# Batch 1's MLP: the leaky slope on ScalarE instead of a product of the weights, and a deeper queue between the products

## The chip, the core and the metric

The kernel runs on one core of one Trainium2 chip. TensorE (PE) multiplies matrices, VectorE (DVE), ScalarE (ACT) and GpSimd (POOL) work elementwise, SyncE (SP) issues most of the DMAs. Times are device microseconds (us) of one execution; less is better.

## The reference

Two steps follow one another: a long convolution, gated by x, and an MLP with a leaky slope.

```python
# 2 batches, seq 12480, d_model 128
h_filt = (np.maximum(pos_emb @ w1, 0.0) @ w2) * np.exp(-0.01 * pos)[:, None]
u = x * v
L = 2 * S
y = np.fft.irfft(np.fft.rfft(u, n=L, axis=1) * np.fft.rfft(h_filt, n=L, axis=0)[None], n=L, axis=1)[:, :S, :]
attn = x * y
# MLP, d_ff 2048, over all 24960 tokens
h = attn.reshape(B * S, D) @ w_in
out = np.maximum(0.01 * h, h) @ w_out
```

## The kernel before

The convolution is a transform of two stages, written as matrix products, with the spectra of batch 0, of batch 1 and of the filter made on the chip. Batch 0's transforms come first (to about 360 us). From then on PE runs the MLP; batch 1's transforms are cut into small pieces (`conv1`, a generator) that the MLP's loop calls between its steps during batch 0's blocks. All of them have run by the time that batch 1's first block begins. The last step of each transform back is made tile by tile in `front(t)`: a tile has 390 tokens, and there are 32 for each batch. `join(t)` makes the sum and the difference cp of what was loaded (L500, L501, on POOL), `front(t)` transposes x (L708), copies it (xs, L710, ACT), multiplies by the last matrix (yp, L716, PE), gates (zf, L719, DVE) and splits the result into two parts, zh (rounded to fp32r, L724, ACT) and zl (the residual, L725, POOL).

The MLP goes over 50 blocks of tokens, 25 for each batch, most of 512 columns (`widths`; batch 1's last two have 352), and over 16 slices of d_ff in each. `m1(k, f)` makes the hidden slice: three passes in fp32r, w_in_h by zh, w_in_h by zl, w_in_l by zh, into one of three PSUM buffers mh. ACT takes the Relu to rh (L737), DVE the residual rl (L738), both from mh. `m2(k, f, r)` adds three more passes to the block's accumulator acc. The slope is not applied elementwise: since max(0.01 h, h) is 0.99 relu(h) + 0.01 h, the kernel keeps 0.99 w_out as w_out_h and w_out_l, and the product wc = 0.01 w_in w_out, and each block begins its accumulator with three passes of z by wc (L748 to L750). `weights()` makes these in the stage before the MLP.

The order is written out by hand. PE gets `m1` of a slice and, DEEP slices later, its `m2`:

```python
pend.append((k, f, m1(k, f)))
if len(pend) > DEEP:
    m2(*pend.pop(0))
```

DEEP is 2, and rh and rl have DEEP + 2 buffers. The steps of `join` and `front` are tied to slices by `ends`: the last part of a tile's front stands behind slice 13 of the block ahead of the one that needs it, or earlier. `finish(k)` copies acc, transposes it back and stores it during the next block. Every engine carries out its instructions in this order.

The matrix of the last-but-one step is held twice: mi2 for batch 0, and mi for batch 1, split once into mi_h and mi_l (L275, L276) in chunk 6 of the first stage. Tiles with the tags bin1, hd and ct1 in the pool sb1 (two, two and one buffers) serve batch 1's transforms.

Of the kernel before, what the change touches and what calls it, by code (L numbers as in the profile page):

```python
# [8 lines left out]
F32 = mybir.dt.float32  # L9
# [3 lines left out]
AF = mybir.ActivationFunctionType  # L13
ALU = mybir.AluOpType
# [10 lines left out]
WIDE = 512  # L25
# [3 lines left out]
def tile_conv_mlp(ctx, tc, x, v, pos_emb, w1, w2, w_in, w_out, cf, cr, cg, cb, ci, cw, out):  # L29
    nc = tc.nc  # L30
    B, S, D = x.shape
# [22 lines left out]
    w_out_h = const.tile([128, NF, D], F32R, name="w_out_h")  # L54
# [50 lines left out]
    def run(g):  # L105
        for _ in g:
            pass
# [50 lines left out]
    with tc.manual_schedule():  # L158
# [17 lines left out]
        def mult_a(c):  # L176
            ft, (xt, vt) = got.pop(c)
            nc.gpsimd.tensor_tensor(out=xt, in0=xt, in1=vt, op=ALU.mult)
            u1[c] = ft, xt

        with ExitStack() as st:
# [4 lines left out]
            mi = s0.tile([128, 2, 128], F32, tag="mi", name="mi", bufs=1)  # L186
# [4 lines left out]
            def load_pos(q):  # L191
                pos_t[q] = sba.tile([NA, 2, PQ, FO], F32, tag="pos", name="pos")
                load_tokens(pos_t[q], pos_emb, q * PQ, PQ)

            def load_a(c):
                ft = sba.tile([NA, MC, 2 * NA], F32, tag="ft", name="ft", bufs=5)
                nc.sync.dma_start(out=ft, in_=cf[:, c * MC:(c + 1) * MC, 0])
                xt = sba.tile([NA, 2, MC, D], F32, tag="xt", name="xt", bufs=3)
                vt = sba.tile([NA, 2, MC, D], F32, tag="vt", name="vt", bufs=3)
                load_tokens(xt, x[0], c * MC, MC)  # L200
                load_tokens(vt, v[0], c * MC, MC)
                f_t[c], xv_t[c] = ft, (xt, vt)
                if c < 2:
                    f1_t[c] = sba.tile([NA, MC, 2 * NA], F32, tag="f1", name="f1", bufs=3)
                    nc.sync.dma_start(out=f1_t[c], in_=cf[:, c * MC:(c + 1) * MC, 1])
# [56 lines left out]
            for c in range(NC0):  # L262
                if c + 3 < NC0:
                    load_a(c + 3)
                    if (c + 3) * MC % PQ == 0:
                        load_pos((c + 3) * MC // PQ)
                if c == 2:
                    nc.sync.dma_start(out=mb, in_=cb)
                    nc.sync.dma_start(out=mi, in_=ci)
                    for s in range(2):  # L270
                        for ri in range(2):
                            nc.sync.dma_start(out=mi2[HB * s:HB * s + HB, ri], in_=ci[HB * ri:HB * ri + HB, s])
                if c == 6:
                    for m, mh, ml in ((mb.rearrange("p s r q -> p s (r q)"), mb_h, mb_l), (mi, mi_h, mi_l)):
                        nc.scalar.copy(mh, m)  # L275
                        nc.vector.tensor_tensor(out=ml, in0=m, in1=mh, op=ALU.subtract)  # L276
                for f in late:
                    f()
                late = []
                uh, ft, f1 = uh_t.pop(c), f_t.pop(c), f1_t.pop(c)  # L280
                nxt = prep(c + 2) if c + 2 < NC0 else iter(())
                o = sba.tile([NA, 2, MC, 2, C0], F32, tag="o", name="o")

                def store(m0, n, o, c=c):
                    for ri in range(2):
                        r0 = HB * ri + c * MC + m0
                        nc.sync.dma_start(out=scr1[r0:r0 + n].rearrange("m k e -> k m e"),
                                          in_=o[:, ri, m0:m0 + n].rearrange("a m s d -> a m (s d)"))
                if c == 7:
                    w22 = s0.tile([128, D], F32, tag="mi", name="w22", bufs=1)  # L290
                    for i in range(2):
                        nc.sync.dma_start(out=w22[64 * i:64 * i + 64, :], in_=w2)
                if c == NC0 - 3:
                    fetch_a(0)

                    bin0 = s0.tile([128, MC1 * 4 * NA], F32, tag="s0", name="bin0", bufs=3)[
                        :, :KC * 2 * C0].rearrange("p (k s e) -> p k s e", k=KC, s=2)

                def early():
                    for ri in range(2):  # L300
                        rows = slice(HB * ri, HB * ri + HB - DIR * MC)
                        nc.sync.dma_start(out=bin0[rows], in_=scr1[rows, :KC, :].rearrange("p k (s e) -> p k s e", s=2))

                def direct(m, o, c=c):
                    for ri in range(2):
                        r0 = HB * ri + c * MC + m
                        nc.sync.dma_start(out=bin0[r0:r0 + 1], in_=o[:KC, ri, m])
                if c == NC0 - 1:
                    mult_a(0)
                for mm in range(MC):  # L310
                    a = psa.tile([NA, 2, 512], F32, tag="a", name="a", bufs=3)
                    for p, f, n in ((0, ft, NA), (1, f1, ROWS)):
                        for ri in range(2):
                            nc.tensor.matmul(a[:, p, C0 * ri:C0 * ri + C0], f[:n, mm, NA * ri:NA * ri + NA],  # L314
                                             uh[:n, p, mm], start=True, stop=True)
                    run(add_sub(sba, a[:, 0, :2 * C0], a[:, 1, :2 * C0], o[:, :, mm, 0, :], o[:, :, mm, 1, :],
                                lambda t: t.rearrange("a (r e) -> a r e", r=2), 2))
                    next(nxt, None)
                    if c >= NC0 - DIR:
                        direct(mm, o)  # L320
                    if c == NC0 - 1 and mm == EARLY:
                        early()
                    if c == NC0 - 1 and mm == MC - 1:
                        store(0, MC, o)
                if c < NC0 - 1:
                    late.append(lambda store=store, o=o: store(0, MC, o))
# [3 lines left out]
        psc = {}  # L330
# [136 lines left out]
        ld, z, acc = {}, {}, {}  # L467
# [36 lines left out]
        with ExitStack() as st:  # L504
# [73 lines left out]
            def two(tag):  # L578
                return [psb.tile([128, 512], F32, tag=tag, name=tag + "p", bufs=2) for _ in range(2)]
# [36 lines left out]
            for c in range(NCH):  # L616
# [16 lines left out]
                hp = two("h")  # L633
                for ri in range(2):
                    for k in range(n):
                        i, j = 64 * (k % 2), ri * n // 2 + k // 2
                        nc.tensor.matmul(hp[k % 2][:, D * j:D * j + D], es[i:i + 64, k // 2, ri, :], w22[i:i + 64, :],
                                         start=True, stop=True)
# [41 lines left out]
        ps = ctx.enter_context(tc.tile_pool(name="ps", bufs=1, space=bass.MemoryType.PSUM, reuse_waits="tile"))  # L680
# [11 lines left out]
        at0 = [sum(widths[:i]) for i in range(len(widths) + 1)]  # L692
# [34 lines left out]
        def m1(k, f):  # L727
            w = widths[k]
            zh, zl = (i[:, :w] for i in z[k])
            hp = ps.tile([128, WIDE], F32, tag="mh", name="mh", bufs=3)[:, :w]  # L730
            fs = slice(f * 128, f * 128 + 128)
            nc.tensor.matmul(hp, w_in_h[:, fs], zh, start=True, stop=False)  # L732
            nc.tensor.matmul(hp, w_in_h[:, fs], zl, start=False, stop=False)  # L733
            nc.tensor.matmul(hp, w_in_l[:, fs], zh, start=False, stop=True)  # L734
            rh = sm.tile([128, WIDE], F32R, tag="rh", name="rh", bufs=DEEP + 2)[:, :w]
            rl = sm.tile([128, WIDE], F32R, tag="rl", name="rl", bufs=DEEP + 2)[:, :w]
            nc.scalar.activation(out=rh, in_=hp, func=AF.Relu)  # L737
            nc.vector.scalar_tensor_tensor(out=rl, in0=hp, scalar=0.0, in1=rh, op0=ALU.max, op1=ALU.subtract)  # L738
            return rh, rl

        def m2(k, f, r):
            rh, rl = r
            w = widths[k]
            if f == 0:
                zh, zl = (i[:, :w] for i in z[k])
                acc[k] = ps.tile([128, WIDE], F32, tag="acc", name="acc", bufs=2)
                ap = acc[k][:, :w]
                nc.tensor.matmul(ap, wc_h, zh, start=True, stop=False)  # L748
                nc.tensor.matmul(ap, wc_h, zl, start=False, stop=False)
                nc.tensor.matmul(ap, wc_l, zh, start=False, stop=False)  # L750
            ap = acc[k][:, :w]
            nc.tensor.matmul(ap, w_out_h[:, f, :], rh, start=False, stop=False)  # L752
            nc.tensor.matmul(ap, w_out_h[:, f, :], rl, start=False, stop=False)  # L753
            nc.tensor.matmul(ap, w_out_l[:, f, :], rh, start=False, stop=(f == NF - 1))  # L754

# [28 lines left out]
                r0 = n + ROWS * NB + 2 * mp  # L784
                nc.sync.dma_start(out=out[None, r0:r0 + 2, :], in_=os_[ROWS:, 0])

        ZB, DEEP = 3, 2

        first = [next(pieces_of(t))[0] for t in range(total)]
        ends, e = {}, NTL * NF  # L790
# [68 lines left out]
        for q in pend:  # L859
            m2(*q)  # L860
# [69 lines left out]
```

## Time and profile before

| | us |
|---|---|
| median of 3 runs | 1763.5 |
| lowest and highest run | 1760.52, 1767.96 |
| profiled execution | 1763.3 |
| its span, first to last instruction | 1761.5 |
| PE busy | 1691.1 (96%) |
| DVE busy | 924.5 (52%) |
| ACT busy | 862.2 (49%) |
| POOL busy | 566.5 (32%) |

Busy times are summed over the span, and the share that PE is busy rises from the transforms at the start to the MLP. Matmuls overlap one another, so a busy PE says only that one was always under way. The rest of the time between span and execution lies outside the first and the last instruction.

### The profile page before, as it was taken

The page shows a single profiled execution, that of the slowest core. Times are in us where ns is not written, and L with a number is a line of the kernel's source. Part 1 is how long each engine was busy: PE and PEld are TensorE (multiplying, and loading weights), DVE is VectorE, ACT ScalarE, POOL GpSimd, SP SyncE. Part 2 cuts the span into 40 slices and gives each one's busy share as a digit, 9 for nine tenths or more (in the row PEclk, how much of TensorE's full clock was granted, in tenths as well). Part 3 has the DMA queues.
Part 4 walks back from the last instruction along what each step waited for, and adds up shares of the span by engine and source line. Part 5 has one row for each costly group of instructions (what it writes and reads, how often), then busy time and mean ns, then how long its engine had stood idle before and what let it go on. Part 6 is the DMA issues. An engine that isn't in the chain of part 4 may idle for free.

```text
span 1761.5 us, 25712 instructions
## 1 busy us (share of the span) xinstructions
PE 1691.1 (96%) x9234; PEld 1398.1 (79%) x9234; DVE 924.5 (52%) x1487; ACT 862.2 (49%) x1673; POOL 566.5 (32%) x474
## 2 busy tenths in 40 slices
PE   6788999699999999999999999999999999999998
PEld 5687555488888888888888888988888888888888
DVE  3566788545454555565555554444444444444444
ACT  1222455234444466667666665444444444444444
POOL 3453122223322166566555653121112111202110
PEclk9889999889999999999999999999999999999999
DMA  8898999766656565656555642221212121212110
GB/s 226 244 269 256 325 327 342 255 179 185 178 150 178 134 176 142 173 150 176 165 140 144 168 131 88 67 70 47 61 50 69 46 59 56 64 38 72 51 30 19
DMA packets 147683, 251.04 MB, mean 143 GB/s; under 512 B 10835, under 2 KB 96930, under 8 KB 144484
## 3 DMA queue, kind: packets, MB, share of 16 engines
q1 hardware_dynamic: 127412, 223.71, 45.4%
q10 hardware_dynamic: 20144, 25.69, 4.1%
q8 instruction: 73, 1.20, 0.3%
q14 instruction: 54, 0.44, 0.1%
HBM read 165.86 MB, written 83.43 MB: 142 GB/s over the span
## 4 chain that ended last, share of the span: by engine, by line
PE 77%; DMA 9%; DVE 6%; issue 3%; SPq 2%; POOL 1%; ACT 1%; ACTq 0%; DVEq 0%; POOLq 0%
PE mh L732 10%; PE acc L753 10%; PE acc L754 10%; PE acc L752 9%; PE mh L734 9%; PE mh L733 9%; PE yp L716 6%; PE cv L132 4%; PE cv L351 2%; DMA scr<-o 2%; PE op L776 2%; DVE ta L126 1%; PE a L314 1%; DMA ft<-in_cf_dram 1%; PE xp L708 1%
## 5 line engine op out<-in xcount | busy, mean ns | idle before, releaser
L738 DVE SCALAR_TENSOR_TENSOR rl<-mh,rh 128x512 fp32r<-128x512 f32 (+3 forms) x800 | 540.7, 678 | 614.7 <-ACT rh L737 612.0
L737 ACT ACTIVATE rh<-mh 128x512 fp32r<-128x512 f32 (+3 forms) x800 | 470.2, 589 | 374.1 <-PE mh L734 352.2
L732 PE MATMUL mh<-zh,w_in_h 128*128 128x512 f32 (+3 forms) x800 | 327.1, 409 | 0.0
L753 PE MATMUL acc<-rl,w_out_h 128*128 128x512 f32 (+3 forms) x800 | 309.9, 387 | 1.4 <-DVE rl L738 1.4
L752 PE MATMUL acc<-rh,w_out_h 128*128 128x512 f32 (+3 forms) x800 | 310.8, 389 | 0.3 <-ACT rh L737 0.3
L734 PE MATMUL mh<-zh,w_in_l 128*128 128x512 f32 (+3 forms) x800 | 310.3, 388 | 0.0
L754 PE MATMUL acc<-rh,w_out_l 128*128 128x512 f32 (+3 forms) x800 | 310.1, 388 | 0.0
L733 PE MATMUL mh<-zl,w_in_h 128*128 128x512 f32 (+3 forms) x800 | 309.3, 387 | 0.2 <-DVE zl L725 0.2
L725 POOL TENSOR_TENSOR zl<-zf,zh 128x390 fp32r<-128x390 f32 (+24 forms) x110 | 67.9, 630 | 700.3 <-ACT zh L724 699.8
L753 PEld LDWEIGHTS acc<-rl,w_out_h 128*128 128x128 f32 x800 | 150.6, 188 | 36.6 <-DVE rl L738 5.5
L734 PEld LDWEIGHTS mh<-zh,w_in_l 128*128 128x128 f32 x800 | 150.6, 188 | 31.8
L752 PEld LDWEIGHTS acc<-rh,w_out_h 128*128 128x128 f32 x800 | 150.7, 188 | 31.5 <-ACT rh L737 1.4
L754 PEld LDWEIGHTS acc<-rh,w_out_l 128*128 128x128 f32 x800 | 150.6, 188 | 30.8
L733 PEld LDWEIGHTS mh<-zl,w_in_h 128*128 128x128 f32 x800 | 151.1, 189 | 23.9 <-DVE zl L725 0.4
L732 PEld LDWEIGHTS mh<-zh,w_in_h 128*128 128x128 f32 x800 | 151.0, 189 | 22.5
L716 PEld LDWEIGHTS yp<-g,cp 98*128 98x128 f32 x1024 | 124.4, 192 | 6.4 <-POOL cp L500 1.2
L716 PE MATMUL yp<-g,cp 98*128 98x97 f32 (+1 forms) x1024 | 123.6, 274 | 1.0 <-POOL cp L500 0.9
L724 ACT CAST zh<-zf 128x390 fp32r<-128x390 f32 (+24 forms) x111 | 37.6, 378 | 156.0 <-DVE zf L719 156.0
L500 POOL TENSOR_TENSOR cp<-cin 98x512 f32<-98x512 f32 x63 | 84.4, 1339 | 17.0 <-DMA cin<-scr 17.0
L99 ACT COPY a1s<-a 98x384 f32<-98x384 f32 x64 | 30.7, 480 | 111.7 <-PE a L314 67.9
L314 PE MATMUL a<-uh,ft 98*98 98x192 f32 x256 | 61.7, 370 | 24.5 <-DVE o L103 21.4
L438 POOL TENSOR_TENSOR usp<-usp,hd 128x512 f32<-128x512 f32 (+1 forms) x50 | 65.3, 1307 | 60.0 <-ACT usp L436 41.9
(127 smaller groups left out, 2109.3 us busy)
## 6 DMA issues: line engine op xcount, KB each, us to landing
cin<-scr SPq DMA_DIRECT2D x64, 392.0 KB
hd<-hspec SPq DMA_DIRECT2D x48, 512.0 KB
g<-in_cg_dram SPq DMA_DIRECT2D x65, 300.1 KB
scr<-o SPq DMA_DIRECT2D x32, 588.0 KB
bin<-scr SPq DMA_DIRECT2D x23, 768.0 KB
scr1b<-o SPq DMA_DIRECT2D x32, 392.0 KB
xm<-in_x_dram SPq DMA_DIRECT2D x65, 192.0 KB
hspec<-hs ACTq DMA_DIRECT2D x48, 256.0 KB
```

Source lines behind the costliest of these rows:

```text
L132: nc.tensor.matmul(dst, u, w, start=(i == 0), stop=(i == 2))
L314: nc.tensor.matmul(a[:, p, C0 * ri:C0 * ri + C0], f[:n, mm, NA * ri:NA * ri + NA], uh[:n, p, mm], start=True, stop=True)
L500: eng.tensor_tensor(out=o1, in0=c0, in1=c1, op=ALU.subtract)
L716: nc.tensor.matmul(yp[:, at:at + n], ci_t[:, r, m, p, :], g[:, r, p, m, :n], start=(r == 0), stop=(r == 1))
L732: nc.tensor.matmul(hp, w_in_h[:, fs], zh, start=True, stop=False)
L733: nc.tensor.matmul(hp, w_in_h[:, fs], zl, start=False, stop=False)
L734: nc.tensor.matmul(hp, w_in_l[:, fs], zh, start=False, stop=True)
L737: nc.scalar.activation(out=rh, in_=hp, func=AF.Relu)
L738: nc.vector.scalar_tensor_tensor(out=rl, in0=hp, scalar=0.0, in1=rh, op0=ALU.max, op1=ALU.subtract)
L752: nc.tensor.matmul(ap, w_out_h[:, f, :], rh, start=False, stop=False)
L753: nc.tensor.matmul(ap, w_out_h[:, f, :], rl, start=False, stop=False)
L754: nc.tensor.matmul(ap, w_out_l[:, f, :], rh, start=False, stop=(f == NF - 1))
```

## The change

For the 25 blocks of batch 1 (`at0[k] >= S`) the three passes over wc go, and the first pass of `m2` opens the accumulator. ACT makes the leaky result itself, r = Lrelu(mh) with slope 0.01, as float32 into SBUF; r is rounded to rh by DVE for odd slices and by ACT for even ones, and DVE subtracts rh from r for rl. The five buffers for r are those of the tags bin1, hd, ct1, bin1, hd in turn. Since w_out_h and w_out_l hold 0.99 w_out, z of batch 1 has to be larger by 1/0.99, and mi is scaled by that once on ACT before it is split. Batch 0's blocks keep Relu, rl from mh and the passes over wc. DEEP goes from 2 to 3 for all blocks: three blocks of passes stand between the two products of a slice in place of two, and rh and rl get one more buffer each.

```diff
                 if c == 6:
+                    nc.scalar.mul(mi, mi, 1 / 0.99)
                     for m, mh, ml in (...):
...
-            nc.scalar.activation(out=rh, in_=hp, func=AF.Relu)
-            nc.vector.scalar_tensor_tensor(out=rl, in0=hp, scalar=0.0, in1=rh, op0=ALU.max, op1=ALU.subtract)
+            if at0[k] < S:
+                nc.scalar.activation(out=rh, in_=hp, func=AF.Relu)
+                nc.vector.scalar_tensor_tensor(out=rl, in0=hp, scalar=0.0, in1=rh, op0=ALU.max, op1=ALU.subtract)
+            else:
+                tag = ("bin1", "hd", "ct1", "bin1", "hd")[f % 5]
+                r = psc["pool"].tile([128, 2048 if tag == "hd" else 1024], F32, tag=tag, name="r",
+                                     bufs=1 if tag == "ct1" else 2)[:, :w]
+                nc.scalar.activation(out=r, in_=hp, func=AF.Lrelu, alpha=0.01)
+                if f % 2:
+                    nc.vector.tensor_copy(rh, r)
+                else:
+                    nc.scalar.copy(rh, r)
+                nc.vector.tensor_tensor(out=rl, in0=r, in1=rh, op=ALU.subtract)
             return rh, rl
...
             if f == 0:
+                acc[k] = ps.tile([128, WIDE], F32, tag="acc", name="acc", bufs=2)
+            if f == 0 and at0[k] < S:
                 zh, zl = (i[:, :w] for i in z[k])
-                acc[k] = ps.tile([128, WIDE], F32, tag="acc", name="acc", bufs=2)
                 ap = acc[k][:, :w]
                 nc.tensor.matmul(ap, wc_h, zh, start=True, stop=False)
                 nc.tensor.matmul(ap, wc_h, zl, start=False, stop=False)
                 nc.tensor.matmul(ap, wc_l, zh, start=False, stop=False)
             ap = acc[k][:, :w]
-            nc.tensor.matmul(ap, w_out_h[:, f, :], rh, start=False, stop=False)
+            nc.tensor.matmul(ap, w_out_h[:, f, :], rh, start=(f == 0 and at0[k] >= S), stop=False)
...
-        ZB, DEEP = 3, 2
+        ZB, DEEP = 3, 3
```

## Rows read from the trace of the kernel before

**Rows 1.** The page's busy us, share of the span and instructions of each engine.
```profile
PE 1691.1 (96%) x9234; PEld 1398.1 (79%) x9234; DVE 924.5 (52%) x1487; ACT 862.2 (49%) x1673; POOL 566.5 (32%) x474
```

**Rows 2.** Windows: us, busy PE, PEld, DVE, ACT, POOL, clock, DMA share, GB/s.
```profile
600.00:1050.00 450.00, 448.31 (x2173) 368.59 (x2172) 248.86 (x348) 297.60 (x574) 258.14 (x212) 1.00 0.61 161
...
1121.10:1738.40 617.30, 617.30 (x3102) 518.74 (x3101) 280.35 (x415) 290.60 (x554) 108.07 (x114) 1.00 0.19 53
```

**Rows 3.** The same window for line 738 alone (DVE).
```profile
1121.10:1738.40 617.30, 263.40 (x385) 1.00 0.19 53
```

**Rows 4.** Waits of PE, 361 to 1122: us in total, times, longest.
```profile
PE acc L753 <- DVE rl L738: 1.4, 6, 0.4
```

**Rows 5.** Timeline of PE at a block's start in batch 1: start, us.
```profile
1384.86 0.39 PE L748 MATMUL acc<-zh,wc_h 128*128 128x512 f32 x1
...
1386.23 0.39 PE L732 MATMUL mh<-zh,w_in_h 128*128 128x512 f32 x1
```

**Rows 6.** Timeline of PE, first block of 352 columns: three passes between the two.
```profile
1721.25 0.32 PE L732 MATMUL mh<-zh,w_in_h 128*128 128x352 f32 x1
...
1721.72 0.40 PE L752 MATMUL acc<-rh,w_out_h 128*128 128x512 f32 x1
```

**Rows 7.** Groups by form: busy us, mean ns of one, idle before and releasers.
```profile
L738 DVE SCALAR_TENSOR_TENSOR rl<-mh,rh 128x512 fp32r<-128x512 f32 x736 | 507.6, 691 | 580.0 <-ACT rh L737 577.4
L737 ACT ACTIVATE rh<-mh 128x512 fp32r<-128x512 f32 x736 | 440.6, 600 | 350.0 <-PE mh L734 328.3 <-DVE rl L738 10.0 <-DVE usp L434 3.2
L399 DVE TENSOR_TENSOR tl<-bin,th 128x512 fp32r<-128x512 f32 x48 | 54.2, 1141 | 2.2 <-ACT th L394 2.2
...
L398 ACT CAST th<-bin 128x512 fp32r<-128x512 f32 x24 | 14.9, 622 | 0.0
...
L84 DVE TENSOR_SCALAR fa<-fb 128x256 uint32<-128x256 uint32 x16 | 4.7, 294 | 0.5
```

**Rows 8.** Timelines of DVE and POOL at two places of batch 1's transforms.
```profile
613.23 1.34 DVE L399 TENSOR_TENSOR tl<-bin,th 128x512 fp32r<-128x512 f32 x2
620.52 1.29 POOL L438 TENSOR_TENSOR usp<-usp,hd 128x512 f32<-128x512 f32 x1 [11.16 <-DVE rl L738]
...
751.61 1.30 POOL L500 TENSOR_TENSOR cp<-cin 98x512 f32<-98x512 f32 x1
752.86 1.29 POOL L501 TENSOR_TENSOR cp<-cin 98x512 f32<-98x512 f32 x1
...
751.74 2.97 DVE L399 TENSOR_TENSOR tl<-bin,th 128x512 fp32r<-128x512 f32 x1
```

**Rows 9.** Timeline behind the front of one tile in batch 1.
```profile
1404.91 0.39 PE L734 MATMUL mh<-zh,w_in_l 128*128 128x512 f32 x1
...
1405.28 0.61 ACT L724 CAST zh<-zf 128x294 fp32r<-128x294 f32 x2 [2.52 <-DVE zf L719]
...
1405.80 1.02 POOL L725 TENSOR_TENSOR zl<-zf,zh 128x294 fp32r<-128x294 f32 x2 [22.19 <-ACT zh L724]
1405.80 0.59 ACT L737 ACTIVATE rh<-mh 128x512 fp32r<-128x512 f32 x1
...
1406.77 1.31 POOL L500 TENSOR_TENSOR cp<-cin 98x512 f32<-98x512 f32 x1
...
1408.04 1.29 POOL L501 TENSOR_TENSOR cp<-cin 98x512 f32<-98x512 f32 x1
```

**Rows 10.** Timeline of ACT at the start; the span's one table load.
```profile
0.74 1.28 ACT L232 ACT_TABLE_LOAD   x1 [0.74 <-PEq L912]
```

**Rows 11.** Timeline of ACT where mi is split.
```profile
77.83 0.41 ACT L275 CAST mi_h<-mi 128x256 fp32r<-128x256 f32 x1
78.89 0.48 ACT L99 COPY a1s<-a 98x384 f32<-98x384 f32 x1 [0.65 <-PE a L314]
```

**Rows 12.** Timeline of PE, the last slice's second product.
```profile
1755.17 0.32 PE L752 MATMUL acc<-rh,w_out_h 128*128 128x352 f32 x1
1755.48 0.43 PE L753 MATMUL acc<-rl,w_out_h 128*128 128x352 f32 x1
```

## The prediction, made before the changed kernel had run

> **What bounds the kernel now.** I read the views from the whole to the detail. The page's busy line [rows 1] has TensorE (PE) at 96% of the span and no other engine above 52%. That alone says little, because the stages differ, so I cut the span where batch 1's first block begins and where its last begins, which holds 24 of its 25 blocks. In that window of 617.3 us [rows 2] PE is busy 617.30 us at a granted clock of 1.00 (2.4 GHz), while VectorE (DVE) has 280 us, ScalarE (ACT) 291 us and GpSimd (POOL) 108 us. The reader is to see that PE never pauses there: batch 1's MLP takes exactly as long as its passes. A pass taken out there shortens the span by its interval, as long as the other engines still keep up. In the stage before it, the view of waits [rows 4] shows PE waiting 1.4 us in six places for the residual rl. So the question has two halves: how much PE work goes, and whether the new work on ACT and DVE can stall PE.
>
> **Passes that go.** Batch 1 has 25 blocks, 23 of 512 columns and 2 of 352, and each loses its three passes over wc. A PE row's duration (0.39 us) overlaps its neighbour's, so the price is the distance between starts. L748, the first pass over wc in one block, starts at 1384.86, and six passes on L732 starts at 1386.23 [rows 5]. That is 1.37 / 6 = 0.228 us for one pass, 0.685 us for three. At 352 columns three passes take 1721.72 - 1721.25 = 0.47 us [rows 6]. Sum: 23 x 0.685 + 2 x 0.47 = 16.7 us. No row of PE's work is added, and the weight loads that go with the passes lie under their neighbours.
>
> **Work that comes, as load.** In those blocks ACT's Relu from PSUM (0.600 us at 512 columns [rows 7]) becomes an Lrelu from PSUM; the trace has no Lrelu. Below, it costs the Relu's 0.60; above, I allow a second pass, 1.20. I take 0.60, since that is the row with the same operands. For even slices ACT also rounds r to rh: the row L398 has just this (SBUF, 128x512, float32 to fp32r), 0.622 us. DVE's L738 (one operand in PSUM, 0.691 us) becomes a subtraction of two SBUF tiles; L399 is that operation, and undisturbed it takes 0.67 us, two in 1.34, with POOL idle for the 11.16 us up to 620.52 [rows 8]. For odd slices DVE also copies r to rh. No row has a DVE copy of 512; L84, one SBUF source with 256 elements, takes 0.294 us [rows 7]. Between 0.29 and 0.67 us (L399's undisturbed time with two sources) I take 0.43. In the window with its 384 slices (24 blocks; the last block ends outside it) ACT gets 192 x 0.622 = 119 us more, 410 us of the 601 that remain (617.3 less 23 x 0.685 and 0.47), 68%. DVE has 280 - 263 = 17 us of other work [rows 2, 3], plus 384 x 0.67 and 192 x 0.43, 357 us in all, 59%. Neither becomes the bound by load.
>
> **Work that comes, as latency.** With DEEP at 3, six groups of three passes stand between m1 of a slice and its m2. From the start of L734 (1404.91 [rows 9]) to the pass that reads rl are 20 intervals, 4.56 us, so that rl is due at 1409.47. In the same rows ACT is held by two zh casts and starts its L737 at 1405.80, 0.89 us behind. It is slice 14 (fronts end behind slice 13, three ahead of the next block), an even one, so after the change ACT's copy would end near 1405.80 + 0.60 + 0.62 + 0.05 = 1407.07 and the subtraction near 1407.75: 1.7 us to spare. For an odd slice DVE's copy is shorter than ACT's. What is queued behind the waiting subtraction on DVE is the next slice's copy or subtraction, which has its own 1.37 us more. This spare time is the cover of the added work.
>
> **The port that DVE and POOL share.** Here a row speaks against the change. L399 took 0.67 us when POOL was idle but 1.141 us on average [rows 7, 8], and once 2.97 us, from 751.74 to 754.71, while POOL ran L500 and L501 from 751.61 to 754.15 [rows 8]. So a DVE subtraction of two SBUF tiles waits for POOL, at worst for two of its instructions. The present L738, with one side in PSUM, does not show that. After the change 400 subtractions, and perhaps the 200 copies, are open to it. The mean wait in L399's stage is 1.14 - 0.67 = 0.47 us at a POOL load of 258 / 450 = 57%; batch 1's POOL load is 108 / 617 = 17.5% [rows 2], so I estimate 0.14 us on each of 576 instructions, 81 us, DVE 438 of 601 us or 73%. Locally the worst place is behind each front, where POOL runs two zl, then L500 and L501, without a break from 1405.80 to 1409.33 [rows 9]. The subtraction would arrive at 1407.07, inside L500; let in at 1408.08 it ends at 1408.75, still 0.7 us early. If L501 goes first as well, it ends at 1409.33 + 0.67 = 1410.00, 0.53 us late. I take 1 us of such stalls over the batch, and keep 0 and 32 x 0.53 = 17 us as ends.
> The Trainium skill, "SBUF — State Buffer", section "SBUF: two separate sides", says that this port pair is an exclusive lock held for a whole instruction, against DVE operations with two SBUF inputs or in a two-port mode. The trace agrees: L399's 2.97 us spans two whole POOL instructions. By that rule, with the first to come served first, the subtraction goes in behind L500 and the sum stays; by the row of 2.97 us repeated in each tile the sum would be 17 us higher.
>
> **The third block between the products, in batch 0.** There the rule of the order changes too. The six waits for rl are at most 0.4 us each [rows 4]. With DEEP at 3 the m2 that needs rl comes 1.37 us later, but the m1 three slices on, which takes the same one of three mh buffers, now stands ahead of that m2 and waits for the same rl instruction. It stands two passes, 0.46 us, behind where the wait is now. All six waits fit into that: -1.4 us; bounds 0 and -1.4. The extra rh and rl buffers take SBUF, not time.
>
> **Edits at nothing.** The scaling of mi on ACT is like L275's 0.41 us and stands before the next a1s copy, ahead of which ACT is idle 0.65 us [rows 11]: hidden, 0.4 us without that cover. A second activation table load, if Lrelu wants one, is 1.28 us [rows 10] once, under the 1.7 us to spare. In the last block L753 now starts 0.31 us after L752 instead of 0.16, a wait of 0.15 [rows 12]; the deeper queue has three m2 left instead of two, the chain is longer by a copy: 0, between -0.15 and +0.3.
>
> **Sum.** The profiled execution took 1763.3 us (span 1761.5), 0.2 below the median of the runs. 1763.3 - 16.7 - 1.4 + 1.0 = 1746.2, and against the median of 1763.5 some 1746.4. I predict 1746.
>
> **Rivals.**
> (a) DVE becomes the bound, and it ends slower. Mechanism: the lock costs every SBUF-sourced DVE instruction in batch 1 what it cost L399, 1.14 us, copies included. Then DVE has 17 + 576 x 1.14 = 674 us against PE's 601: 73 us over, 1763.3 - 18.1 + 73 = 1818. For it: the mean of L399 is measured. Against: POOL's load is a third of that stage's. It eats the whole gain once the mean of these instructions passes (601 + 18 - 17) / 576 = 1.05 us; I expect 0.73 (0.59 and 0.14). Chance 0.05.
> (b) Both cp instructions pass ahead of the subtraction in every tile: 17 us of stalls instead of 1, 1762, no change. For it the one row of 2.97; against it that L399's mean is far below. Chance 0.07.
> (c) The change does not keep to one table: Relu, copies and Lrelu alternate with loads. The trace has one load in the whole span [rows 10]. Two loads of 1.28 us for each pair of slices make 2.56 us; with ACT's other work for the pair (410 us over 192 pairs, 2.14) that is 4.70 us against PE's 3.13 (601 / 192): 200 x 1.57 = 314 us more, 1763.3 - 18.1 + 314 = 2059. Chance 0.02.
> The Trainium skill, "ScalarE: Activation LUTs", section "Table sets: the hidden batching unit", says that cheap functions such as copies are in every set; no run here shows Lrelu's set.
> (d) Lrelu takes two passes, 1.20 us: ACT has 410 + 384 x 0.6 = 640 us against 601, 39 over, 1784. Chance 0.02.
>
> **How the numbers follow.** Forecast 0.81, (a) 0.05, (b) 0.07, (c) 0.02, (d) 0.02, and 0.03 for stalls between the forecast and (b). The forecast's own ends are the sum without stalls (1745.2) less the 3 us by which the lowest run lay below the median, 1742, and the sum with no gain in batch 0 and the table load paid (1748.9) plus 3, 1752. To leave out no more than 2 in 10 and take in part of the stalls I set 1742 to 1756. A change of 0.5% (8.8 us) is about what a measurement of this kernel can tell from none. Faster by more: the forecast and the 0.03, 0.84. Within: (b), 0.07. Slower: (a), (c), (d), 0.09.
>
> **What would show it.** Right: the window of batch 1's blocks near 601 us with PE busy throughout at clock 1.00, no passes over wc after block 24, no waits for rl in batch 0, the Lrelu row at 0.60, ACT's copy at 0.62, the subtraction between 0.67 and 0.9, DVE's copy near 0.43. Wrong: PE waits at L753's successor for rl, clustered behind POOL's cp instructions (b), a subtraction mean above 1.05 and DVE without idle time (a), many table loads (c), Lrelu near 1.2 (d). A POOL zl held by DVE beyond the new block's first m1 would be a wait that I put at nothing.

## The result and the profile after

Five runs of the changed kernel have a median of 1747.65 us (1745.96 to 1752.0), five of the kernel before 1766.48 us (1760.52 to 1769.36). The ratio on record is 0.991, 95% interval 0.9894 to 0.9925; the quotient of these two medians is 0.989. The forecast was 1746, in a range of 1742 to 1756. The profiled execution took 1745.96 us with a span of 1744.1. Of the runs in the next section one of e10 took 2570.34 us at a mean granted clock of 0.6, and its ratio leaves it out.

The page's busy line, and the windows of the same blocks as in [rows 2], which now begin at 1116.55 and end at 1721.13 (columns: us, busy PE, weight loads, DVE, ACT, POOL, clock, DMA share, GB/s):

```profile
PE 1676.3 (96%) x9159; PEld 1382.8 (79%) x9159; DVE 1058.4 (61%) x1687; ACT 972.3 (56%) x1875; POOL 579.5 (33%) x474
```
```profile
1116.55:1721.13 604.58, 604.55 (x3030) 502.98 (x3029) 408.57 (x606) 396.91 (x747) 120.99 (x114) 1.00 0.19 55
```

PE still never pauses there by this view, at a granted clock of 1.00, and DVE and ACT have a third of the window left. The groups by form that answer to [rows 7], of the same kernel:

```profile
L750 DVE TENSOR_TENSOR rl<-r,rh 128x512 fp32r<-128x512 f32 x368 | 275.7, 762 | 139.0 <-ACT rh L749 132.7
...
L745 ACT ACTIVATE r<-mh 128x512 f32<-128x512 f32 x368 | 220.4, 599 | 121.9 <-PE mh L735 107.8
...
L749 ACT CAST rh<-r 128x512 fp32r<-128x512 f32 x184 | 114.2, 621 | 5.8
...
L747 DVE CAST rh<-r 128x512 fp32r<-128x512 f32 x184 | 110.1, 598 | 29.3 <-ACT r L745 26.6
```

Lrelu costs what Relu did, ACT's copy what L398 did. The two DVE groups have means of 0.762 and 0.598 us. The views of their two lines (duration in ns, minimum, median and maximum; first and last start) have medians of 0.692 and 0.428 us and maxima far above:

```profile
L750 DVE TENSOR_TENSOR rl<-r,rh x400: 524/692/1755, 1119.5 to 1737.5; 128x512 fp32r<-128x512 f32 x123, 128x352 fp32r<-128x352 f32 x11
```
```profile
L747 DVE CAST rh<-r x200: 341/428/1526, 1120.1 to 1737.2; 128x512 fp32r<-128x512 f32 x92, 128x352 fp32r<-128x352 f32 x8
```

So some of these instructions wait for something.

Where the time went, by the starts of the first pass of blocks 0, 1, 25 and 49 in the two traces:

```
                                before    after    difference
ahead of block 0                361.71    362.46     +0.75
block 0                          24.39     21.33     -3.06
blocks 1 to 24 (batch 0)        735.03    732.76     -2.27
blocks 25 to 48 (batch 1)       617.28    604.58    -12.70
block 49 to the end              23.10     23.01     -0.09
span                           1761.51   1744.14    -17.37
```

The first two lines have little to do with the change. Ahead of block 0 the thirteen traces of this document lie between 359.8 and 367.2 us, with and without the change. Block 0 before holds a wait of 0.88 us for the second tile's cp (L500), and behind it some passes start 0.33 us apart instead of 0.18, where the granted clock is 0.50 (1.2 GHz):

```profile
371.84:375.25 3.41, 3.41 (x12) 3.41 (x12) 1.13 (x2) 1.38 (x3) 2.19 (x2) 0.50 0.55 151
```

Three traces have such a stretch inside block 0, this one, e5 and e6 below, and take 24.4 to 24.9 us for it, whatever DEEP is; the ten others take 21.3 to 22.2. Some time is only moved between the lines: with DEEP 3 one m2 fewer stands ahead of each line's end. Block 0 loses 0.53 us by it, and block 49 gains 0.47, which hides its passes over wc; for the two lines between, what comes and what goes differ by 0.1 us at most.

That leaves a surplus and a lack. 24 blocks without their passes should have lost 16.2 us and lost 12.7. The view of waits has two lines for this (the engine and line that waited, what it waited for; us, times, longest), the first from batch 0, the second from batch 1's weight loads:

```profile
PE mh L733 <- DVE rl L740: 0.8, 3, 0.3
...
PEld acc L766 <- DVE rl L750: 8.2, 29, 0.5
```

PE itself shows no wait for rl in batch 1, for a matmul row overlaps the next. It is the weight load ahead of the pass over rl that comes late, 29 times. By their order 22 of these loads are slice 15's and 7 are slice 7's; the seven belong to the tiles whose front ends behind slice 5 instead of 13. One of the 22, in the last block, is late before the change too. Part of each such delay is hidden by the pass that still runs. The timeline behind the front that answers to [rows 9]:

```profile
1395.46 0.39 PE L735 MATMUL mh<-zh,w_in_l 128*128 128x512 f32 x1
...
1395.95 1.30 POOL L501 TENSOR_TENSOR cp<-cin 98x512 f32<-98x512 f32 x1
...
1396.25 1.54 DVE L750 TENSOR_TENSOR rl<-r,rh 128x512 fp32r<-128x512 f32 x1 [1.83 <-ACT rh L749]
...
1397.20 1.75 POOL L502 TENSOR_TENSOR cp<-cin 98x512 f32<-98x512 f32 x1
...
1397.72 1.52 DVE L747 CAST rh<-r 128x512 fp32r<-128x512 f32 x1
...
1399.27 1.30 DVE L750 TENSOR_TENSOR rl<-r,rh 128x512 fp32r<-128x512 f32 x2
...
1399.81 0.40 PE L765 MATMUL acc<-rh,w_out_h 128*128 128x512 f32 x1
...
1400.02 0.19 PEld L766 LDWEIGHTS acc<-rl,w_out_h 128*128 128x128 f32 x1 [0.25 <-DVE rl L750]
1400.05 0.48 PE L766 MATMUL acc<-rl,w_out_h 128*128 128x512 f32 x1
...
1400.36 0.40 PE L767 MATMUL acc<-rh,w_out_l 128*128 128x512 f32 x1
```

Slice 14's subtraction (1396.25) waits for the first cp and ends at 1397.79; the second cp waits for it (1.75 us instead of 1.30); slice 15's copy on DVE (1397.72) waits for that cp and takes 1.52 us; so slice 15's subtraction begins only at 1399.27 and ends near 1399.96. The pass over this rl, 20 intervals behind L735 at 1395.46, starts at 1400.05, nearly on time. But its weight load, which starts one interval ahead of its pass where nothing is late (1398.44 for the pass at 1398.67 in this view), stood idle for 0.25 us, and L767 follows 0.31 us behind L766 instead of 0.23. DVE and POOL take turns here, one instruction each, and so they do in the same order behind all 29 fronts that have this work behind them.

### The profile page after: what moved, and what is told of

Same layout as the page of the kernel before. It is cut to its first block, busy times and chain, and to the rows that moved or that the text cites. A ratio compares the mean times of both kernels' runs of the same rounds, so it can differ in the third digit from the quotient of the medians.

```text
span 1744.1 us, 26079 instructions
## 1 busy us (share of the span) xinstructions
PE 1676.3 (96%) x9159; PEld 1382.8 (79%) x9159; DVE 1058.4 (61%) x1687; ACT 972.3 (56%) x1875; POOL 579.5 (33%) x474
## 4 chain that ended last, share of the span: by engine, by line
PE 80%; DMA 10%; DVE 6%; SPq 1%; issue 1%; ACT 1%; POOL 0%; ACTq 0%; DVEq 0%; POOLq 0%
PE mh L733 10%; PE acc L766 10%; PE acc L765 10%; PE mh L735 10%; PE acc L767 10%; PE mh L734 10%; PE yp L717 7%; PE cv L132 4%; PE cv L352 3%; DMA xt<-in_x_dram 2%; DMA scr<-o 2%; DMA ft<-in_cf_dram 2%; PE op L789 2%; DVE ta L126 1%; PE xp L709 1%; DVE tb L126 1%
## 5 line engine op out<-in xcount | busy, mean ns | idle before, releaser
L740 DVE SCALAR_TENSOR_TENSOR rl<-mh,rh 128x512 fp32r<-128x512 f32 (+2 forms) x400 | 269.1, 677 | 300.3 <-ACT rh L739 296.7
L750 DVE TENSOR_TENSOR rl<-r,rh 128x512 fp32r<-128x512 f32 (+1 forms) x400 | 292.5, 743 | 147.8 <-ACT rh L749 140.8
L733 PE MATMUL mh<-zh,w_in_h 128*128 128x512 f32 (+3 forms) x800 | 328.2, 410 | 0.9 <-DVE rl L740 0.8
L739 ACT ACTIVATE rh<-mh 128x512 fp32r<-128x512 f32 (+2 forms) x400 | 234.9, 590 | 153.1 <-PE mh L735 141.8
L766 PE MATMUL acc<-rl,w_out_h 128*128 128x512 f32 (+3 forms) x800 | 310.7, 388 | 0.0
L735 PE MATMUL mh<-zh,w_in_l 128*128 128x512 f32 (+3 forms) x800 | 310.1, 388 | 0.0
L767 PE MATMUL acc<-rh,w_out_l 128*128 128x512 f32 (+3 forms) x800 | 309.9, 387 | 0.0
L745 ACT ACTIVATE r<-mh 128x512 f32<-128x512 f32 (+1 forms) x400 | 235.4, 589 | 129.3 <-PE mh L735 115.3
L766 PEld LDWEIGHTS acc<-rl,w_out_h 128*128 128x128 f32 x800 | 150.3, 188 | 38.3 <-DVE rl L750 8.2
L735 PEld LDWEIGHTS mh<-zh,w_in_l 128*128 128x128 f32 x800 | 150.6, 188 | 32.1
L767 PEld LDWEIGHTS acc<-rh,w_out_l 128*128 128x128 f32 x800 | 150.3, 188 | 30.4
L733 PEld LDWEIGHTS mh<-zh,w_in_h 128*128 128x128 f32 x800 | 151.2, 189 | 25.0 <-DVE rl L740 3.0
L747 DVE CAST rh<-r 128x512 fp32r<-128x512 f32 (+1 forms) x200 | 115.6, 578 | 31.2 <-ACT r L745 28.4
L749 ACT CAST rh<-r 128x512 fp32r<-128x512 f32 (+1 forms) x200 | 122.0, 610 | 6.3
```

The lines of the kernel that those rows point to most:

```text
L745: nc.scalar.activation(out=r, in_=hp, func=AF.Lrelu, alpha=0.01)
L749: nc.scalar.copy(rh, r)
L750: nc.vector.tensor_tensor(out=rl, in0=r, in1=rh, op=ALU.subtract)
```

## The experiments

Each was timed beside the kernel before on the same chip, e1 to e4 on one chip and e5 to e11 on another. Since the whole times scatter by several us (23 executions of the kernel before, beside e1 to e4, took 1759.96 to 1768.26), much of it ahead of batch 1, the window from the first pass of block 25 to that of block 49 in each trace is what tells small differences:

```
                       window     ratio to before (95% interval)
before                 617.28
changed kernel         604.58     0.991   0.9894 to 0.9925
e1_no_wc               600.94     0.9914  0.9901 to 0.9927
e2_depth_alone         617.30     0.9995  0.9985 to 1.0005
e3_depth_back          644.73     1.0161  1.0147 to 1.0176
e4_wc_kept             620.81     1.0021  1.001  to 1.0032
e5_relu                604.80     0.9914  0.9898 to 0.9929
e6_psum                601.38     0.9909  0.9894 to 0.9925
e7_cp_twice            638.93     1.0117  1.0099 to 1.0135
e8_psum_all            601.10     0.9935  0.9922 to 0.9949
e9_copy15_act          602.00     0.9891  0.9875 to 0.9907
e10_psum_depth2        601.72     0.9897  0.9882 to 0.9913
e11_copies_act         601.01     0.9899  0.9885 to 0.9913
```

**e1_no_wc: the passes alone.** The kernel before with

```diff
-            if f == 0:
+            if f == 0 and at0[k] < S:       # the passes over wc
```

and the accumulator opened by the first product.

> The kernel before without batch 1's three passes over wc and with nothing else changed (its output lacks the 0.01 h part for batch 1). If a pass is worth the distance between starts, the 24 blocks of the window fall from 617.3 us by 23 x 0.685 + 0.47 = 16.2 us to 601.1, the whole by 16.7, and the deeper queue and the new work have no part in it: near 1747 us by the profiled execution's 1763.3. The rival, that the passes gave cover to something that is late next, gives less than 14 us and new waits of PE in batch 1.

The window fell by 16.34 us against the 16.2 expected; the median is 1746.98. A pass is worth the distance between starts here, and nothing new is late behind it: one weight load waits for rl, 0.3 us in the last block, as in the kernel before.

**e2_depth_alone and e3_depth_back: the third block.**

```diff
-        ZB, DEEP = 3, 2
+        ZB, DEEP = 3, 3        # e2, in the kernel before; e3 is the reverse, in the changed one
```

> The kernel before with DEEP 3 alone. My theory: it removes batch 0's waits for rl but for some left at the mh buffers, 0.6 to 1.4 us, and nothing in batch 1, which had no waits: a ratio of 0.999 to 1.000, batch 1's window at 617.3. The rival is what the first profile after shows, 4.6 us less ahead of batch 1, as an effect of the deeper queue: then this run has 4 us less there too (a ratio of 0.997).

> The changed kernel with DEEP back at 2. The rl of a slice is then due 14 intervals or 3.2 us behind the last pass of its first product instead of 4.6. Behind each front the profile after has the subtraction end about 0.1 us late, so it would be late by about 1.5 us there in each of 32 tiles, some 45 us; the waits for copies of other even slices fit in (a chain of 2.4 us). Expected 1746 + 45 + 1 = 1792, slower than the kernel before. The rival, that the third block is not needed, expects 1747.

Alone, DEEP 3 leaves batch 1's window at 617.30 and takes 1.9 us from blocks 1 to 24 (733.17 instead of 735.03); by the whole time it can't be told from nothing. Without it the changed kernel is slower than the kernel before: 1789.39 us, window 40 us longer, where 45 were expected. The weight loads' waits of that run:

```profile
PEld acc L766 <- DVE rl L750: 41.3, 60, 1.0
PEld acc L765 <- DVE rh L747: 12.7, 29, 0.4
```

So the leaky slope alone loses what the passes give and more, and the third block is what makes the change pay.

**e4_wc_kept: the price without the gain.** The changed kernel with the two conditions on `at0[k]` in `m2` taken out.

> The changed kernel with the three passes over wc kept in batch 1 (its output then has the 0.01 h part twice for batch 1). That is the added work on ACT and DVE and the deeper queue without the gain. If gain and price add up, it takes 16.7 us more than the changed kernel, 1746 + 17 = 1763, that is the kernel before plus some 3.5 us of waits behind the fronts less what batch 0 gains. The rival is that the passes hide those waits: then 3 us less, 1760.

The window is 16.23 us above the changed kernel's and 3.5 above that of before: gain and price add up, and the passes hid nothing: 29 weight loads wait for rl as in the changed kernel, 8.3 us in all. The median, 1766.07, is 3 above what I expected of the whole; the window is not.

**e5_relu: function and table.**

```diff
-                nc.scalar.activation(out=r, in_=hp, func=AF.Lrelu, alpha=0.01)
+                nc.scalar.activation(out=r, in_=hp, func=AF.Relu)
```

> The changed kernel with Relu in place of Lrelu in batch 1, all else kept (its output there is 0.99 of relu(h) w_out without the 0.01 h part). Only the second table load of 1.28 us goes and the function's own price. Lrelu and Relu both took 0.60 us at 512 columns, so the time stays: 1746 to 1748, and the block where batch 1 begins shows no gain, since the load lies under the time to spare. The rival, that the load is paid in full, gives 1.3 us less in that block.

The window is 604.80, no less than with Lrelu. The table load is there in the changed kernel, once in batch 1, ahead of its first slice (timeline of ACT), and hidden:

```profile
1116.94 1.28 ACT L745 ACT_TABLE_LOAD   x1
```

**e6_psum and e7_cp_twice: is it the port, or the length of the chain?**

```diff
-                r = psc["pool"].tile(...)
+                r = hp                      # e6: Lrelu in place in PSUM
```
```diff
+            for _ in range(2 if t >= NT else 1):      # e7: join(t), around both cp instructions
```

> The changed kernel with r written back in place into mh in PSUM instead of an SBUF buffer. DVE's subtraction then has one operand in PSUM (as L738 of before, 0.69 us) and its copy reads PSUM. Theory of the shared port: the waits behind POOL's cp go, batch 1's window falls from 604.6 to about 601.1 us, subtraction rows stay below 0.72 us, and the whole is 3.5 us less, near 1743. Rival: the chain of Lrelu, copy and subtraction is too long behind the fronts by itself; it has the same length here, so that PE still waits for rl some 29 times and the window stays at 604.6. A third: mh comes free later, and the first product waits for it, more than 1747.

> The changed kernel with POOL making each cp of batch 1 twice over (the same values again), 2.6 us more of POOL for a tile, off every other engine's chain. Theory of the shared port: behind each front two more DVE instructions wait, about 0.85 us each as in the profile after, and rl comes 0.9 to 1.7 us later than due: 30 to 50 us over 32 tiles, 1776 to 1796. Rival, the chain is too long by itself: POOL has the time (cp is due some 9 us later), so the time stays at 1746 to 1748.

e6 took 3.2 us from the window, and its DVE groups no longer spread (their longest instructions take 0.694 us); cp is back at 1.30 us (two groups by form; waits of the weight loads; timeline of the second cp behind the same front):

```profile
L748 DVE TENSOR_TENSOR rl<-mh,rh 128x512 fp32r<-128x512 f32 x368 | 254.4, 691 | 134.0 <-ACT rh L747 127.7
...
L745 DVE CAST rh<-mh 128x512 fp32r<-128x512 f32 x184 | 126.9, 690 | 41.1 <-ACT mh L743 36.0
```
```profile
PEld acc L764 <- DVE rl L748: 0.3, 1, 0.3
```
```profile
1396.65 1.30 POOL L502 TENSOR_TENSOR cp<-cin 98x512 f32<-98x512 f32 x1
```

The chain is as long as in the changed kernel, and for odd slices longer (a copy of 0.69 us for one of 0.43). The waits are gone but for the one in the last block, so length alone was not the cause. e7 adds work to POOL alone, with no shorter or longer chain, and costs 34 us, 1783.54 in all. The waits of its weight loads, and its timelines of DVE and POOL behind one front:

```profile
PEld acc L767 <- DVE rl L751: 44.8, 47, 1.4
```
```profile
1393.44 1.60 DVE L751 TENSOR_TENSOR rl<-r,rh 128x512 fp32r<-128x512 f32 x1 [1.83 <-ACT rh L750]
1394.97 1.52 DVE L748 CAST rh<-r 128x512 fp32r<-128x512 f32 x1
1396.53 3.36 DVE L751 TENSOR_TENSOR rl<-r,rh 128x512 fp32r<-128x512 f32 x2
```
```profile
1393.20 1.30 POOL L502 TENSOR_TENSOR cp<-cin 98x512 f32<-98x512 f32 x1
1394.46 1.74 POOL L503 TENSOR_TENSOR cp<-cin 98x512 f32<-98x512 f32 x1
1396.16 1.49 POOL L502 TENSOR_TENSOR cp<-cin 98x512 f32<-98x512 f32 x1
1397.61 1.73 POOL L503 TENSOR_TENSOR cp<-cin 98x512 f32<-98x512 f32 x1
```

Four cp, and four DVE instructions that take turns with them. Both runs came out as the theory of the shared port has it.

**e8_psum_all: batch 0's blocks too.** e6 with the conditions on `at0[k]` set for all blocks, and without the factor 0.99, the scaling of mi and the weights' product.

> The step that follows if the place in PSUM holds: all 50 blocks make the leaky result in PSUM, the passes over wc, the product of the weights and the factor 0.99 go altogether. Batch 0 loses 25 x 3 passes too, 16.7 us (its blocks are 390, 512 and 314 columns wide, so 16.5), and the weights' product in the stage before loses some work that is partly hidden. But ACT there is at 298 of 450 us and gets 0.31 us for each slice of some 1.95 us, 82%, DVE 55% and up to 70%. If they keep up: 1743 - 16 = 1727. If ACT's queue between the pieces of batch 1's transforms delays rh, half of that is lost, 1735; above 1743 the load of ACT decides and batch 0 should keep its passes.

A miss: 1752.37 us, above e6. Batch 1's window is the same, but blocks 1 to 24 take 741.44 us where the changed kernel has 732.76, with 16 us of passes less. My reason was wrong as well. In the window 600 to 1050 ACT has 344 of 450 us (76%) and DVE 312 (69%), neither near its limit. The waits of PE in batch 0 name the buffer:

```profile
PE mh L715 <- DVE rl L730: 14.4, 22, 2.1
```

In batch 0 a buffer now comes free only behind three instructions, Lrelu, copy and subtraction, instead of two, and ACT and DVE have the transforms' pieces in their queues as well. That these pieces make it late is argued and not shown. The view accounts for 14.4 of some 25 us lost. The weight loads ahead of the same passes tell more (from block 1 to 24):

```profile
PEld mh L715 <- DVE rl L730: 27.9, 36, 2.5
```

PE also ran at a granted clock of 0.50 (1.2 GHz) from 853.56 to 856.98, behind the start of a pass that had waited 2.07 us; no other trace has such a stretch in these blocks. How the loss divides between the two is not shown.

**e9_copy15_act, e11_copies_act: who makes the copy.**

```diff
-                if f % 2:
+                if f % 2 and f != 15:       # e9; e11 has "if False:"
```

> The changed kernel with the copy of slice 15 on ACT instead of DVE in batch 1's blocks; the other odd slices stay on DVE. In the profile after, the rl that is late behind a front is slice 15's: its copy on DVE waits for the second cp (1.52 us instead of 0.43) and its subtraction stands behind that copy. With ACT's copy ready at 1397.33, the subtraction waits for the same cp until 1399.09 and ends at 1399.76, before 1400.04 where it is due. So the 29 waits go and batch 1's window falls from 604.6 to 601.4, near the place in PSUM. If instead the subtraction of slice 14 or the port at large sets the wait, the window stays at 604 to 605.

> The changed kernel with all copies to rh on ACT in batch 1. ACT goes from some 410 to 529 of 601 us in the window, 88%, DVE loses 83 us and the copies that wait for POOL. If ACT's queue still keeps up: window 601 to 603, as for slice 15 alone. If the pair Lrelu and copy (1.22 us of each 1.37) leaves too little behind the fronts, where two zh casts and two further copies stand in the same queue, rh comes late by 1 us in a tile: 630 and more.

Moving one copy in 16 shortened the window to 602.00 and left 8 of 29 late weight loads, where 601.4 and none were expected; moving all to ACT shortened it to 601.01, with ACT at 507 of 601 us (the waits of e9 and a timeline behind one front, the window of e11):

```profile
PEld acc L766 <- DVE rl L750: 2.5, 8, 0.4
```
```profile
1182.83 1.52 DVE L747 CAST rh<-r 128x512 fp32r<-128x512 f32 x1
...
1185.13 0.19 PEld L766 LDWEIGHTS acc<-rl,w_out_h 128*128 128x128 f32 x1 [0.35 <-DVE rl L750]
```
```profile
1120.71:1721.72 601.01, 601.01 (x3030) 505.14 (x3029) 330.62 (x415) 507.10 (x938) 121.06 (x114) 1.00 0.20 55
```

Of the 8, 7 are slice 7's, behind the fronts that end at slice 5, and there e9 left the copy on DVE (1.52 us again, at 1182.83); the eighth is the one in the last block. All of slice 15's in the window are gone. So the instruction that made rl late was the copy on DVE behind each front. ACT's queue kept up at 84%.

**e10_psum_depth2: what the third block pays for.** e6 with DEEP 2.

> r in place in PSUM, and DEEP back at 2. Without the port, the chain from the last pass of the first product is 0.39 + 0.60 + 0.62 + 0.69 and gaps, 2.4 us, and behind a front 0.5 us more for the zh casts: 2.9 against the 3.2 that two blocks give. Expected window 601 to 604, where the changed kernel with DEEP 2 took 644.7: the third block pays for the port's waits, not for the chain. Rival: the chain needs the third block also without the port; then the window is above 620.

The window is 601.72, against 644.73 for the changed kernel with DEEP 2. Away from the port, two blocks are enough; 4 weight loads still wait, 1.4 us in all.

By the windows e6, e9, e10 and e11 take 2.6 to 3.6 us less than the changed kernel. All four are faster than the kernel before by some 1%; their intervals overlap that of the changed kernel, so that the whole time doesn't settle which of the five is best.

## Why the prediction was right, point by point

- **Passes that go:** 16.2 us of the 16.7 lie in the window, and e1 measured 16.34 there. Shown.
- **Load:** ACT 397 us in the window instead of 410, DVE 409 instead of 357 without and 438 with the estimate for the port. Lrelu 0.599, ACT's copy 0.621, DVE's copy 0.428 in the median (0.43 was chosen between 0.29 and 0.67 with no row of that form, so that the hit is luck). Rival (a), DVE as the bound, needed a mean of 1.05 us for DVE's instructions; the means are 0.762 and 0.598. Rival (d) fell with the Lrelu row, (c) with one table load.
- **The port:** the term that was mis-sized. I took 1 us, and the window shows 16.3 - 12.7 = 3.6 us, 0.13 in each of its 28 places. The mechanism was the stated one, and e6 and e7 show it. I followed the wrong instruction: slice 14's subtraction got in behind the first cp and was in time, as forecast by turns. What I passed over with "its own 1.37 us more" was slice 15, whose copy on DVE meets the second cp and whose subtraction stands behind it. e9 shows this by moving that copy alone. For the tiles whose front ends behind slice 5 the same holds of slice 7. I also set the deadline at the pass over rl; by that slice 15's subtraction, over near 1399.96, was in time for 1400.02 (1395.46 and 4.56). The weight load one interval ahead is what came late.
- **Who goes next:** rival (b), both cp ahead of the subtraction in every tile, did not come. DVE and POOL took turns, each until the other's instruction was over (1.52 us for a copy of 0.43, 1.75 for a cp of 1.30), and the copy with one SBUF source waits too. The exclusive lock that the Trainium skill, "SBUF — State Buffer", section "SBUF: two separate sides", describes agrees with these rows.
- **The third block:** -1.4 us forecast for batch 0; e2 has -1.9 and the changed kernel -2.3 in blocks 1 to 24, the remaining 0.8 us of waits at mh, where I put them. Single traces scatter there: the four with DEEP 2 take 735.0 to 736.4 us (mean 735.7), the eight with DEEP 3 other than e8 732.5 to 735.1 (mean 733.5). So the means differ by 2.2 us, more than the 1.4 that I set as the bound: I read PE's waits alone, and the weight loads for rh and rl stood idle 6.6 us in these blocks before (L752, L753), and those that wait for rl 3.0 after (L733). That it also decides the sign of the change I had in the numbers (1.7 us to spare behind a front, of which the third block gives 1.37) but did not say; e3 shows it.
- **Edits at nothing:** the table load was hidden (e5). The scaling of mi is hidden too: it takes 0.42 us on ACT, and the a1s copy behind it still finds ACT idle 0.30 us, waiting for PE, where it was 0.65 [rows 11]:

```profile
76.58 0.42 ACT L274 ACTIVATE mi<-mi 128x256 f32<-128x256 f32 x1
...
77.90 0.48 ACT L99 COPY a1s<-a 98x384 f32<-98x384 f32 x1 [0.30 <-PE a L315]
```

- **Sum:** -17.1 was forecast for the profiled execution and -17.3 measured, by terms that err both ways: the port 2.6 us more, batch 0 0.9 less, and 2.3 less from block 0 and ahead of it, of which 0.5 is the m2 moved to block 1 and the rest, by the thirteen traces, not the change's. The 0.4 left over is the m2 moved to block 49. That the sum came out so near is luck in part.

## What to carry to other kernels

Where PE is the bound and never pauses, price a pass by the distance between starts and take it out; then spend the argument on whether the work put in its place stays in time. When an elementwise operation on VectorE moves from PSUM to SBUF operands, look at what GpSimd runs at that moment, and follow not only the instruction that meets it but the ones queued behind. A deeper queue between two products can be worth nothing by itself and still decide whether another change pays.

## What the runs showed of the hardware that was not expected

DVE's copy of 512 float32 from SBUF to fp32r took 0.428 us undisturbed and 0.690 from PSUM (e6), so that the form that waits for GpSimd is also the faster one. DVE and GpSimd alternated one instruction at a time behind every front where both had work. A slightly late operand shows in the row of the weight load and not in that of the matmul: 29 loads sat idle 8.2 us in all, and the window lost 3.6. Where it is later, in e3, the matmul's row has waits too, 18.9 us in 58 places beside 41.3 at the loads.
